# Transposing x by crossbar DMA instead of on TensorE, in a two-stage attention and MoE kernel

## Chip, cores and metric

The kernel runs on one core of one Trainium2 chip. The metric is the device time of one execution in microseconds (us), given as the median of a few runs. A profile is one further execution, recorded by the hardware profiler.

## The reference

Attention against 32 inducing points in two steps, then a dense expert layer with a hard swish. The four batches have 12480 rows of 128 channels each; the hidden width of the expert layer is 2048.

```python
B, N, m, C = (4, 12480, 32, 128)
scale = 1.0 / np.sqrt(C)
I = np.broadcast_to(inducing[None], (B, m, C))

def mab(q, kv):
    s = scale * (q @ kv.transpose(0, 2, 1))
    s = s - s.max(-1, keepdims=True)
    a = np.exp(s)
    a /= a.sum(-1, keepdims=True) + 1e-09
    return a @ kv
h = mab(I, x)               # 32 rows per batch, gathered from all of x
y = mab(x, h)               # every row of x looks at the 32 rows
# expert layer on the B*N rows of y: d_model 128, d_ff 2048
hid = y @ w_in
g = hid * np.clip(hid + 3.0, 0.0, 6.0) / 6.0
out = (g @ w_out).astype(np.float32)
```

## The kernel before

**The work.** Each batch of x is cut into seven groups: six of 128 x 16 rows (512 KB once they are bf16, 1 MB as fp32) and a last one of 48 x 4 rows. A group holds four chunks of 512 rows (the last group one), so a batch has 25 chunks. For each batch there are three parts:

- *a*, over groups: read x, cast it to bf16 (`a_cast`, L251, ScalarE, two halves per group), transpose it on TensorE in two halves into PSUM (`a_T`, L260) and copy that to the long bf16 tile `xT` on VectorE (L261), compute the scores against the inducing points and their exponentials (`a_s1`, L268 and L274), and add the weighted rows into `hnd` (`a_agg`, L282).
- *c*, once per batch: turn the 32 gathered rows into coefficients of the output stage (`c_units`: L470, L481, L490 and others).
- *b*, over chunks: for every row exponentials against coefficients (`b_base`, L652 and L659), a product with the tile `d` (`b_prod`, L668), 16 matmuls per chunk (`b_quad`, L692), one more (`b_lin`, L676), a row factor (`b_r`, L612 and L613), and the scaled result (`b_evac`, L708), which is stored once per group (L715). The tile `d` of a chunk comes from a packed tile `dk` of its group by a small DMA that copies 32 partitions to 128 (`b_spread`, L639).

**The order.** It is written by hand (`manual_schedule`), so each engine runs its instructions in the order in which the program emits them. Batch 0's parts *a* and *c* run first (`a_first`, `c_first`). Then a loop runs over all 100 chunks; while it does part *b* of batch b it takes small pieces of parts *a* and *c* of batch b+1 from a list. The list is filled at the first chunk of a batch, by `a_units(b + 1)` followed by `c_units(b + 1)`, and emptied evenly over 25 chunks: three times per chunk `bg(part)` takes as many units as the share of the chunks done asks for. For batch 1 four empty units stand ahead. So parts *a* of batches 1, 2 and 3 fall into the first third or so of the loop over batches 0, 1 and 2. A full group has five units: first half of the transposes with half of the next group's cast, half of the aggregation of the group before, second half of the transposes with the other half of the cast, the rest of the aggregation, and the scores. The casts of a batch's group 0 are emitted near the end of the batch before.

**Queues.** Loads of x and of the weights are issued by GpSimd (L118, L149 to L152). The spreads of `d` (L639, emitted four chunks ahead of their output and used by `b_prod` three loop turns later) and the outputs (L715) are issued by SyncE (SP). A load of x waits until its fp32 buffer (five of them) is free.

**Buffers.** `xT` has two tiles (one per batch in turn), the bf16 copy `xb` two (one per group in turn), `d` four. The PSUM tile of the transposes comes from `psF`, five banks that most of the work shares (for batch 0 it alternates with `psO`).

**The end.** Counts taken on the way say whether the fast form of the computation was valid. If not, a slow direct path runs under `tc.If` (L818 to L822). With the inputs given it doesn't run: every engine loads the flag, branches at L821 and goes past its instructions.

Of the kernel before, what the change touches and what calls it, by code (L numbers as in the profile page):

```python
# [9 lines left out]
FP32 = mybir.dt.float32  # L10
# [30 lines left out]
def kernel(  # L41
# [8 lines left out]
    nc = tc.nc  # L50
    P = nc.NUM_PARTITIONS
    B, N, C = x.shape
# [4 lines left out]
    scale = 1.0 / math.sqrt(C)  # L57


    groups = []  # L60
    t0 = 0
# [14 lines left out]

    keep = ctx.enter_context(tc.tile_pool(name="keep", bufs=1))
    bad_i = keep.tile([1, 1], I32, name="bad_i")

    with ExitStack() as es:  # L80
        es.enter_context(tc.manual_schedule())
# [70 lines left out]
            nc.gpsimd.dma_start(w_out_r[:, :, :], w_out)  # L152


        ident = const.tile([P, P], FP32, name="ident")
        make_identity(nc, ident[:, :])
        for g in range(1, XBUF):
            load_x(0, g)
# [94 lines left out]
        def a_T(b, g, h):  # L253
# [6 lines left out]
                nc.tensor.transpose(pt[:, (i - lo) * p : (i - lo + 1) * p], xb[:p, i, :], ident_b[:p, :p])  # L260
            nc.vector.tensor_copy(st["xT"][:, t0 + lo * p : t0 + hi * p], pt[:, : (hi - lo) * p])  # L261

        def a_s1(b, g):
            t0, p, n = groups[g]
            st = S[b]
            s1 = side_bank(b, [P, 512], FP32, "s1")
            for i in range(n):
                nc.tensor.matmul(  # L268
                    s1[:p, i * M : (i + 1) * M],
                    lhsT=st["xT"][:, t0 + i * p : t0 + (i + 1) * p],  # L270
                    rhs=I_T[:, :],
                )
# [29 lines left out]

        def a_units(b):

            us = []
            late = []
            for g in range(NGR):
                box = {}

                def s1_unit(g=g, box=box):  # L310
                    a_s1(b, g)
                    box["a1"] = S[b]["a1"]

                def first(g=g):
                    a_T(b, g, 0)
                    if g + 1 < NGR:
                        a_cast(b, g + 1, ((nc.scalar.copy, 0, 2),))

                def second(g=g):
                    a_T(b, g, 1)  # L320
                    if g + 1 < NGR:
                        a_cast(b, g + 1, ((nc.scalar.copy, 2, 4),))

                us.append(first)
                if late:
                    us.append(late.pop(0))
                us.append(second)
                us += late
                us.append(s1_unit)
                late = [  # L330
                    lambda g=g, box=box: a_agg(b, g, 0, box["a1"]),
                    lambda g=g, box=box: a_agg(b, g, 1, box["a1"]),
                ]
            return us + late
# [484 lines left out]
        bad_i[0:1, 0:1], min_val=0, max_val=1, skip_runtime_bounds_check_because="a comparison gives 0 or 1"  # L819
    )  # L820
    with tc.If(bad > 0, preferred_fallthrough_block=False):  # L821
        direct_path(tc, x, inducing, moe_w_in, moe_w_out, out, scale)  # L822


def direct_path(tc, x, inducing, moe_w_in, moe_w_out, out, scale):
    nc = tc.nc
    P = nc.NUM_PARTITIONS
    B, N, C = x.shape
# [7 lines left out]
    with ExitStack() as es:  # L836
        kp = es.enter_context(tc.tile_pool(name="d_keep", bufs=1))
        wk = es.enter_context(tc.tile_pool(name="d_work", bufs=1))
        ps = es.enter_context(tc.tile_pool(name="d_ps", bufs=1, space=PSUM))
        ident = kp.tile([P, P], FP32, name="d_ident")  # L840
        make_identity(nc, ident[:, :])
        w_in = kp.tile([P, F], FP32, name="d_w_in")
        nc.sync.dma_start(w_in[:, :], moe_w_in[:, :])
        w_out = kp.tile([P, FB, C], FP32, name="d_w_out")
# [19 lines left out]
            nc.tensor.matmul(s[:M, :TN], lhsT=I_T[:, :], rhs=xT[:, :])  # L864
            return s

        for b in range(B):
            mx = kp.tile([M, 1], FP32, name="d_mx")
            nm = kp.tile([M, 1], FP32, name="d_nm")
            D = kp.tile([M, 1], FP32, name="d_D")  # L870
            Ha = kp.tile([M, C], FP32, name="d_Ha")
            HT = kp.tile([P, M], FP32, name="d_HT")
            nc.vector.memset(mx[:, :], -3.0e38)
            nc.vector.memset(D[:, :], 0.0)
            nc.vector.memset(Ha[:, :], 0.0)
            with tc.For_i(b * N, (b + 1) * N, TN) as row:
                xt, xT = load(row)
                s = weights_of(xT)
                m1 = wk.tile([M, 1], FP32, name="d_m1")
                nc.vector.tensor_reduce(m1[:, :], s[:M, :TN], axis=AX.X, op=ALU.max)  # L880
                nc.vector.tensor_max(mx[:, :], mx[:, :], m1[:, :])
            nc.vector.tensor_scalar_mul(nm[:, :], mx[:, :], -scale)
            with tc.For_i(b * N, (b + 1) * N, TN) as row:
                xt, xT = load(row)
                s = weights_of(xT)
                a = wk.tile([M, TN], FP32, name="d_a")
                nc.scalar.activation(a[:, :], s[:M, :TN], ACT.Exp, scale=scale, bias=nm[:, 0:1])
                d1 = wk.tile([M, 1], FP32, name="d_d1")
                nc.vector.tensor_reduce(d1[:, :], a[:, :], axis=AX.X, op=ALU.add)
                nc.vector.tensor_add(D[:, :], D[:, :], d1[:, :])  # L890
                tr = ps.tile([P, 512], FP32, name="d_tr")
                nc.tensor.transpose(tr[:TN, :M], a[:, :], ident[:M, :M])
                aT = wk.tile([TN, M], FP32, name="d_aT")
                nc.vector.tensor_copy(aT[:, :], tr[:TN, :M])
                hp = ps.tile([P, 512], FP32, name="d_h")
                nc.tensor.matmul(hp[:M, :C], lhsT=aT[:, :], rhs=xt[:, :])
                nc.vector.tensor_add(Ha[:, :], Ha[:, :], hp[:M, :C])
            nc.vector.tensor_scalar_add(D[:, :], D[:, :], 1.0e-9)
            nc.vector.reciprocal(D[:, :], D[:, :])
            nc.vector.tensor_scalar_mul(Ha[:, :], Ha[:, :], D[:, 0:1])  # L900
            tr = ps.tile([P, 512], FP32, name="d_tr")
            nc.tensor.transpose(tr[:, :M], Ha[:, :], ident[:M, :M])
            nc.vector.tensor_copy(HT[:, :], tr[:, :M])
            with tc.For_i(b * N, (b + 1) * N, TN) as row:
                xt, xT = load(row)
                s = ps.tile([P, 512], FP32, name="d_s")
                nc.tensor.matmul(s[:TN, :M], lhsT=xT[:, :], rhs=HT[:, :])
                m2 = wk.tile([TN, 1], FP32, name="d_m2")
                nc.vector.tensor_reduce(m2[:, :], s[:TN, :M], axis=AX.X, op=ALU.max)
                nc.vector.tensor_scalar_mul(m2[:, :], m2[:, :], -scale)  # L910
                a = wk.tile([TN, M], FP32, name="d_a2")
                nc.scalar.activation(a[:, :], s[:TN, :M], ACT.Exp, scale=scale, bias=m2[:, 0:1])
                d2 = wk.tile([TN, 1], FP32, name="d_d2")
                nc.vector.tensor_reduce(d2[:, :], a[:, :], axis=AX.X, op=ALU.add)
                nc.vector.tensor_scalar_add(d2[:, :], d2[:, :], 1.0e-9)
                nc.vector.reciprocal(d2[:, :], d2[:, :])
                nc.vector.tensor_scalar_mul(a[:, :], a[:, :], d2[:, 0:1])
# [22 lines left out]
                nc.sync.dma_start(out[bass.ds(row, TN), :], ot[:, :])  # L940


# [28 lines left out]
```

## Time and profile before

| | us |
|---|---|
| runs: median (lowest to highest) of 3 | 327.13 (325.17 to 327.18) |
| profiled execution | 323.27 |
| its span, first to last instruction | 321.5 |
| TensorE busy | 299.8 |
| VectorE busy | 237.5 |
| ScalarE busy | 229.4 |
| ScalarE casts of full groups (L251), 42 | 43.4 |
| VectorE copies of transposes (L261), 48 full ones | 32.2 |
| TensorE transposes (L260), 384 full ones, by record | 29.4 |

The busy time of an engine is the time in which at least one of its instructions is on record as running; matmuls overlap in the records, so the sum of their single times is more than the time that they hold TensorE. PE stands for TensorE, PEld for its weight loads, DVE for VectorE, ACT for ScalarE, POOL for GpSimd and SP for SyncE; a q behind the name means its instruction queue (waits, branches, DMA issues). A row of a group reads "line engine operation out<-in count | busy us, mean ns". The loop over chunks starts at about 46 us; batches 0, 1 and 2 take 74, 74 and 73 us of it, and batch 3, beside which nothing is prepared, 46 us. The last output is issued at 313.77 us.

### The profile page before, as it was taken

The page shows a single profiled execution, that of the slowest core. Times are in us where ns is not written, and L with a number is a line of the kernel's source. Part 1 is how long each engine was busy: PE and PEld are TensorE (multiplying, and loading weights), DVE is VectorE, ACT ScalarE, POOL GpSimd, SP SyncE. Part 2 cuts the span into 40 slices and gives each one's busy share as a digit, 9 for nine tenths or more (in the row PEclk, how much of TensorE's full clock was granted, in tenths as well). Part 3 has the DMA queues.
Part 4 walks back from the last instruction along what each step waited for, and adds up shares of the span by engine and source line. Part 5 has one row for each costly group of instructions (what it writes and reads, how often), then busy time and mean ns, then how long its engine had stood idle before and what let it go on. Part 6 is the DMA issues. An engine that isn't in the chain of part 4 may idle for free.

```text
span 321.5 us, 9629 instructions
## 1 busy us (share of the span) xinstructions
PE 299.8 (93%) x3934; PEld 234.7 (73%) x3934; DVE 237.5 (74%) x542; ACT 229.4 (71%) x416; POOL 23.3 (7%) x59
## 2 busy tenths in 40 slices
PE   7798998999999998999899998999999999999980
PEld 2695756888677877888678777898777777777760
DVE  2688677788876768788786767797895777878780
ACT  2481789986689669986589759887589757777630
POOL 8150110201000000110000000100000000000000
PEclk9599999999999999999999999999999999999996
DMA  7999399898946444799965345652455246666652
GB/s 222 420 276 272 76 386 329 281 307 285 406 115 197 149 151 98 196 357 332 322 203 181 117 106 178 177 181 77 137 187 191 68 139 210 204 207 197 199 218 75
DMA packets 26487, 67.78 MB, mean 211 GB/s; under 512 B 5153, under 2 KB 19521, under 8 KB 20289
## 3 DMA queue, kind: packets, MB, share of 16 engines
q1 hardware_dynamic: 18160, 38.36, 37.1%
q0 software_dynamic: 8272, 28.71, 29.1%
q8 instruction: 33, 0.54, 0.7%
q14 instruction: 22, 0.17, 0.2%
HBM read 29.77 MB, written 25.56 MB: 172 GB/s over the span
## 4 chain that ended last, share of the span: by engine, by line
PE 75%; DMA 11%; DVE 6%; ACT 3%; issue 2%; POOL 0%; DVEq 0%; POOLq 0%
PE op L692 26%; PE bp L652 12%; DMA d<-dk 8%; PE op L676 6%; PE hnd L282 6%; PE pt L260 5%; PE cp L490 4%; PE dpm L470 4%; DMA xr<-in_x_dram 4%; PE s L268 3%; PE pp L623 2%; DVE xT L261 2%; PE sp L593 2%; PE ep L579 2%; DVE TD L668 1%
## 5 line engine op out<-in xcount | busy, mean ns | idle before, releaser
L659 ACT ACTIVATE TF<-bp 128x512 bf16<-128x512 f32 (+1 forms) x200 | 117.9, 600 | 34.8 <-PE rp L612 21.2
L692 PE MATMUL op<-Cq,TF 128*128 128x128 bf16 (+1 forms) x800 | 109.2, 223 | 0.0
L692 PE MATMUL op<-Cq,TD 128*128 128x128 bf16 (+1 forms) x800 | 106.3, 219 | 0.7 <-DVE TD L668 0.5
L708 DVE TENSOR_TENSOR os<-op,r_all 128x512 f32<-128x512 f32 (+1 forms) x100 | 68.2, 682 | 20.1 <-PE op L692 19.2
L692 PEld LDWEIGHTS <-TF 128*128 128x128 bf16 (+1 forms) x800 | 50.7, 98 | 33.5 <-issue 25.4
L652 PE MATMUL bp<-xT,W 128*128 128x512 bf16 (+1 forms) x200 | 75.1, 376 | 0.0
L668 DVE TENSOR_TENSOR TD<-TF,d 128x1024 bf16<-128x1024 bf16 (+1 forms) x100 | 66.8, 668 | 5.2 <-DMA d<-dk 2.5
L692 PEld LDWEIGHTS <-TD 128*128 128x128 bf16 (+1 forms) x800 | 61.4, 98 | 1.2 <-DVE TD L668 1.0
L676 PE MATMUL op<-BD,nf 128*128 128x512 f32 (+1 forms) x100 | 53.1, 531 | 0.0
L251 ACT CAST xb<-xr 128x1024 bf16<-128x1024 f32 (+1 forms) x47 | 46.0, 1002 | 7.1 <-DMA xr<-in_x_dram 7.1
L481 ACT ACTIVATE sq<-dpm 128x512 bf16<-128x512 f32 x60 | 36.5, 645 | 5.6 <-PE dpm L470 3.7
L261 DVE COPY xT<-pt 128x1024 bf16<-128x1024 bf16 (+1 forms) x56 | 33.8, 616 | 7.6 <-PE pt L260 7.5
L613 DVE RECIPROCAL r_all<-rp 128x4 f32<-128x4 f32 (+1 forms) x100 | 17.7, 177 | 23.9 <-PE rp L612 23.5
L612 PE MATMUL rp<-one,nf 128*128 128x4 f32 (+1 forms) x100 | 34.3, 343 | 0.1
L260 PE MATMUL pt<-ident_b,xb 128*128 128x128 bf16 (+1 forms) x400 | 31.0, 223 | 2.0 <-DVE xb L251 1.5
L282 PE MATMUL hnd<-xr,a 128*32 128x128 f32 x384 | 31.8, 229 | 0.5 <-ACT a L274 0.5
L282 PEld LDWEIGHTS hnd<-xr,a 128*32 128x32 f32 x384 | 25.6, 111 | 2.7 <-issue 2.1
L260 PEld LDWEIGHTS <-xb 128*128 128x128 bf16 (+1 forms) x400 | 24.6, 100 | 3.9 <-DVE xb L251 1.6
L118 POOL DMA_DIRECT2D xr<-in_x_dram x25 | 13.5, 543 | 161.8 <-ACT TF L659 94.4
L490 PE MATMUL cp<-w_out_b,sq 128*128 128x128 bf16 x256 | 24.3, 220 | 0.4 <-ACT sq L481 0.4
L470 PE MATMUL dpm<-dH,w_in_b 128*128 128x512 bf16 x64 | 23.7, 381 | 0.9 <-DVE dH L400 0.5
L630 ACT ACTIVATE dk<-pp 128x512 bf16<-128x512 f32 (+1 forms) x28 | 15.8, 564 | 11.5 <-PE pp L623 10.5
(106 smaller groups left out, 343.7 us busy)
## 6 DMA issues: line engine op xcount, KB each, us to landing
out_dram<-os SPq DMA_DIRECT2D x24, 1024.0 KB, 4.2
xr<-in_x_dram POOLq DMA_DIRECT2D x23, 1024.0 KB, 7.8
d<-dk SPq DMA_DIRECT2D x96, 128.0 KB, 4.1
xr<-in_x_dram POOLq DMA_DIRECT2D x2, 512.0 KB, 4.7
w_in_r<-in_moe_w_in_dram POOLq DMA_DIRECT2D x1, 1024.0 KB, 10.1
w_out_r<-in_moe_w_out_dram POOLq DMA_DIRECT2D x1, 1024.0 KB, 14.4
w_in_b<-in_moe_w_in_dram POOLq DMA_DIRECT2D x1, 512.0 KB, 6.8
w_out_b<-in_moe_w_out_dram POOLq DMA_DIRECT2D x1, 512.0 KB, 12.3
```

Source lines behind the costliest of these rows:

```text
L251: eng(xb[:p, lo:hi, :], xs[(b, g)][:p, lo:hi, :].bitcast(FP32))
L260: nc.tensor.transpose(pt[:, (i - lo) * p : (i - lo + 1) * p], xb[:p, i, :], ident_b[:p, :p])
L261: nc.vector.tensor_copy(st["xT"][:, t0 + lo * p : t0 + hi * p], pt[:, : (hi - lo) * p])
L282: nc.tensor.matmul(st["hnd"][:M, :C], lhsT=a1[:p, i * M : (i + 1) * M], rhs=xs[(b, g)][:p, i, :], start=(g == 0 and i == 0), stop=(g == NG ...
L470: nc.tensor.matmul(dpm[:, :], lhsT=w_in_b[:, jb * P : (jb + 1) * P], rhs=st["dH"][:, :, :, :, :].rearrange("p q k m i -> p (q k m i)"),)
L490: nc.tensor.matmul(st["cp"][:, k * C : (k + 1) * C], lhsT=sq[:, k * P : (k + 1) * P], rhs=w_out_b[:, jc, :], start=(jc == 0 and k == 0), s ...
L652: nc.tensor.matmul(bp[:, :w], lhsT=st["W"][:, k].rearrange("p m i -> p (m i)"), rhs=st["xT"][:, c0 : c0 + w],)
L659: nc.scalar.activation(st[("x", c)][:, k, :w], bp[:, :w], ACT.Exp, scale=scale)
L668: nc.vector.tensor_mul(u[:, :, :w], t[:, :, :w], d[:, :w].unsqueeze(1).to_broadcast([P, 2, w]))
L676: nc.tensor.matmul(op[:p, :], lhsT=st[("nf", g)][:, j * p : (j + 1) * p], rhs=st["BD"][:, :], start=True, stop=False, skip_group_check=True,)
L692: nc.tensor.matmul(op[:p, s * C : (s + 1) * C], lhsT=T[k][:, s * p : (s + 1) * p], rhs=st["Cq"][:, k, :], start=False, stop=(s == SL - 1 a ...
L708: nc.vector.tensor_mul(ot[:p, j * SL : (j + 1) * SL, :], op[:p, :].rearrange("p (s c) -> p s c", c=C), r_all[:p, b, c, :].unsqueeze(2).to_ ...
```

## The change

For batches 1 to 3, `a_T` and its copies are no longer called. A new function `a_X` issues one DMA per group on SP that reads the bf16 copy, transposes it in the DMA crossbar and writes `xT` directly. The transfer of group g+1 is issued in the unit that computes the scores of group g; that of group 0 is the batch's first unit, with two empty units behind it. The halves of the casts become units of their own. A batch has 83 units instead of 80. Batch 0 keeps its transposes on TensorE.

The direct path at the end is written with a loop over batches instead of four copies of its body, and it uses the identity matrix of the main path, which moves to the pool that outlives it, instead of making its own.

```diff
     keep = ctx.enter_context(tc.tile_pool(name="keep", bufs=1))
     bad_i = keep.tile([1, 1], I32, name="bad_i")
+    ident = keep.tile([P, P], FP32, name="ident")
...
-        ident = const.tile([P, P], FP32, name="ident")
         make_identity(nc, ident[:, :])
...
+        def a_X(b, g):
+
+            t0, p, n = groups[g]
+            nc.sync.dma_start(
+                S[b]["xT"][:, t0 : t0 + n * p].rearrange("c (i p) -> c i p", p=p),
+                xbs[(b, g)][:p, :n, :].rearrange("p i c -> p (i c)"),
+                transpose=True,
+            )
+
...
-            us = []
+            us = [lambda: a_X(b, 0), lambda: None, lambda: None]
             late = []
             for g in range(NGR):
                 box = {}
...
                 def s1_unit(g=g, box=box):
                     a_s1(b, g)
                     box["a1"] = S[b]["a1"]
-
-                def first(g=g):
-                    a_T(b, g, 0)
                     if g + 1 < NGR:
-                        a_cast(b, g + 1, ((nc.scalar.copy, 0, 2),))
-
-                def second(g=g):
-                    a_T(b, g, 1)
+                        a_X(b, g + 1)
+
+                for h in (0, 2):
                     if g + 1 < NGR:
-                        a_cast(b, g + 1, ((nc.scalar.copy, 2, 4),))
-
-                us.append(first)
-                if late:
-                    us.append(late.pop(0))
-                us.append(second)
-                us += late
+                        us.append(lambda g=g, h=h: a_cast(b, g + 1, ((nc.scalar.copy, h, h + 2),)))
+                    if late:
+                        us.append(late.pop(0))
                 us.append(s1_unit)
...
-        direct_path(tc, x, inducing, moe_w_in, moe_w_out, out, scale)
+        direct_path(tc, x, inducing, moe_w_in, moe_w_out, out, ident, scale)
...
-        ident = kp.tile([P, P], FP32, name="d_ident")
-        make_identity(nc, ident[:, :])
...
-        for b in range(B):
+        with tc.For_i(0, B * N, N) as r0:
...
-            with tc.For_i(b * N, (b + 1) * N, TN) as row:
-                xt, xT = load(row)
+            with tc.For_i(0, N, TN) as row:
+                xt, xT = load(r0 + row)
```

(The last four lines stand for the three loops of the direct path, which change alike.)

More of the change, by code (lines that the diff above doesn't have):

```diff
@@ L821, with direct_path @@
     with tc.If(bad > 0, preferred_fallthrough_block=False):
-        direct_path(tc, x, inducing, moe_w_in, moe_w_out, out, scale)
-def direct_path(tc, x, inducing, moe_w_in, moe_w_out, out, scale):
+        direct_path(tc, x, inducing, moe_w_in, moe_w_out, out, ident, scale)
+def direct_path(tc, x, inducing, moe_w_in, moe_w_out, out, ident, scale):
     nc = tc.nc
@@ L882, in direct_path @@
             nc.vector.tensor_scalar_mul(nm[:, :], mx[:, :], -scale)
-            with tc.For_i(b * N, (b + 1) * N, TN) as row:
-                xt, xT = load(row)
+            with tc.For_i(0, N, TN) as row:
+                xt, xT = load(r0 + row)
                 s = weights_of(xT)
@@ L903, in direct_path @@
             nc.vector.tensor_copy(HT[:, :], tr[:, :M])
-            with tc.For_i(b * N, (b + 1) * N, TN) as row:
-                xt, xT = load(row)
+            with tc.For_i(0, N, TN) as row:
+                xt, xT = load(r0 + row)
                 s = ps.tile([P, 512], FP32, name="d_s")
@@ L939, in direct_path @@
                 nc.vector.tensor_copy(ot[:, :], op[:TN, :C])
-                nc.sync.dma_start(out[bass.ds(row, TN), :], ot[:, :])
+                nc.sync.dma_start(out[bass.ds(r0 + row, TN), :], ot[:, :])
 _INS = ['x', 'inducing', 'moe_w_in', 'moe_w_out']
```

## The prediction, made before the changed kernel was run

> **What bounds the kernel now.** I read the page's busy rows first, then a table of stretches, then the chain of waits inside one stretch, then the queue that carries the new transfers.
>
> ```profile
> PE 299.8 (93%) x3934; PEld 234.7 (73%) x3934; DVE 237.5 (74%) x542; ACT 229.4 (71%) x416; POOL 23.3 (7%) x59
> ...
> DMA  7999399898946444799965345652455246666652
> ```
>
> TensorE leads, but these are averages. The loop works on batch b and prepares b+1 in its first third, so the second view is the stretches in which batches 1, 2 and 3 are prepared (columns: length, busy time and count of PE, PEld, DVE, ACT, POOL, granted clock, DMA share, GB/s).
>
> ```profile
> 52.00:76.00 24.00, 23.99 (x388) 20.67 (x389) 18.98 (x38) 20.97 (x34) 2.67 (x5) 1.00 0.87 273
> 127.00:150.00 23.00, 23.00 (x377) 19.64 (x376) 18.73 (x39) 18.74 (x32) 2.98 (x6) 1.00 0.83 272
> 201.00:230.00 29.00, 28.64 (x443) 23.86 (x442) 23.38 (x51) 21.76 (x37) 1.03 (x2) 1.00 0.50 154
> ```
>
> TensorE has no gap in any of them. ScalarE is next: 20.97/24, 18.74/23 and 21.76/29, or 87, 81 and 75%. VectorE stands at 79 to 81%. The DMA engines are crowded in the first two (0.87, 0.83), where x is loaded, and half free in the third. The chain of waits shows what TensorE does there.
>
> ```profile
> 128.79 0.39 PE s L268 x16
> 129.18 0.23 PE op L692 x4
> 129.41 0.45 PE pt L260 x8
> 129.86 0.22 PE bp L652
> ...
> 131.75 0.45 PE pt L260 x8
> ```
>
> Every piece starts where the last ends: this is issue-bound TensorE, so an instruction taken out here is time. Eight transposes cost 0.45 us (56 ns each), not the 225 ns that a single record shows, since records overlap. From the timeline, the scores (L268) of five full groups of the third stretch start at 202.69, 207.96, 212.99, 217.60 and 223.29: 5.15 us per group. Last, the transfers.
>
> ```profile
> out_dram<-os SPq DMA_DIRECT2D x24, 1024.0 KB, 4.2
> xr<-in_x_dram POOLq DMA_DIRECT2D x23, 1024.0 KB, 7.8
> d<-dk SPq DMA_DIRECT2D x96, 128.0 KB, 4.1
> ```
>
> SP's queue carries the spread of d and the outputs; the transposes join both there.
>
> **What the Trainium skill says.** DMA: Bandwidth & Descriptors, section Latency and other measured facts, gives a DMA transpose 261 GB/s with a non-contiguous middle dimension and 350 to 400 GB/s contiguous. No transfer of this trace is a transpose, so it neither agrees nor differs. The same page, section Issuing engines are not separate DMA queues, says that transfers of all issuers run on the same 16 engines. The trace agrees: with loads from POOL and spreads from SP both open the DMA share is 0.87. Runtime: NRT & Kernel Launch, section Instruction fetch mechanics, says that a taken branch with its target outside the fetched window waits for a fetch. The trace agrees:
>
> ```profile
> L821 PEldq COMPARE_BRANCH  x2: 95/1948/3801, 314.5 to 314.8; - x2
> ...
> L966 POOLq DRAIN  x3: 50/107/2832, 317.8 to 321.2; - x3
> ```
>
> The jump over the unused direct path takes TensorE 3.8 us, and ten instruction packets are moved after 315 us. POOL takes its branch at 314.5 and starts its drain at 317.8.
>
> **The change, part by part.**
>
> *Transposes off TensorE.* Per batch six groups of 16 and one of four go, 100 in all: 100 x 56 ns = 5.6 us, 16.8 us for three batches. Their waits go too, and two psF banks per group stay free. What is late next is ScalarE. A stretch of about 30 us would shrink to 24.4, and ScalarE works about 0.81 x 30 = 24.3 us in it: the two meet. At the start of each stretch ScalarE already leads (4.48 of 4.50 us at 122 to 126.5, TensorE 3.58), so the gain isn't whole. I take 4.0 us per batch, 12 us in all; the ends are 2.5 and 5.6.
>
> *Copies off VectorE.* Twelve L261 copies at 685 ns and two at 202 ns go per batch, 8.6 us. VectorE isn't the bound, so this counts nothing by itself; it also removes the handover TensorE to VectorE to TensorE ahead of the scores.
>
> *Casts on ScalarE.* The same two per group, 1.04 us each, now in units of their own. No time. The bf16 slot (two of them) is freed when its transfer has landed instead of when TensorE has read it.
>
> *The transfers.* Seven per batch on SP: six of 512 KB, one of 48 KB. Each waits on SP for the two casts of its group; spreads and outputs queue behind it. The wait itself should be nothing: the cast of one group ended at 206.90, and its scores' place in TensorE's order is at 212.99, so a transfer has 5 to 6 us, or 4.5 to 5.5 when groups come faster. If TensorE stalls on one group, the casts of the next don't depend on that, so two can be in flight. The latency: a spread of 128 KB landed in 2.5 us at the least, and its 128 packets of 1 KB at 46 ns fill 16 engines for 0.37 us, so 2.1 us are fixed. The data of 512 KB: bounded below by the spread's rate, 4 x 0.37 = 1.5 us; bounded above by the slowest kind of packet of the same size as a source row of a 128 x 128 block, 256 B, where w_out_b's load shows 41 ns each: 2048 x 41 / 16 = 5.2 us. I take the skill's 261 GB/s, 2.0 us, because it is the one figure for the same operation. Quiet landing: 2.1 + 2.0 = 4.1 us, hidden. Beside a load, with half the engines' turns, 6.1 us; behind a 1 MB output (128 KB takes 0.37 us, the output 2.6 us) 8.7 us. Two outputs and six groups fall in each stretch. In the two crowded ones I count one group 3.5 us late and the others saved by what is ahead, less what the stall lets ScalarE catch up: 2.5 us lost per crowded batch, 5 us in all; the ends are 0 and 12. In the third nothing is late.
>
> *The spread of d behind the transfers.* It is issued three chunks before VectorE needs it, some 9 us. Median landing 4.1 us leaves 5 us of cover for a transfer ahead of it (2 to 4 us). The cover is thin in one place: a spread issued at 149.55 took 9.40 us and was waited for. I put that inside the 5 us above. How long SP itself is held by one transpose the trace doesn't show: at least the 0.54 us of a spread's issue, at most the whole data time; by the same cover either costs nothing until it passes 5 us.
>
> *First transfer of a batch.* It is issued in the first unit and used six units later (a unit is 73.5 us / 80 = 0.92 us): 5.5 us, hidden. Batch 1's has four empty units more, which it needs, since 46 to 54 us run at a DMA share above 1. The 83 units for 80 only pack the third two thirds of the loop denser.
>
> *The short direct path.* It isn't executed. One loop body stands for four, so the jump lands nearer. Without any fetch, POOL's drain would begin 3.2 us sooner; I take 2.0 us, ends 0 and 3.3. The identity made once in another pool is made at the same place: nothing.
>
> *Sum.* -12 + 5 - 2 = -9 us, against the profiled execution's 323.27: 314.3 us. The median of the runs, 327.13, stands 1.2% above that execution; the same step from it gives 327.13 x 314.3 / 323.27 = 318.0 us. Changes below 1% (3.3 us) can't be told from none here.
>
> **Rivals.**
>
> *A, the forecast:* transfers mostly hidden, ScalarE next: 318.0 us, its own range 312 to 322.
>
> *B, gain eaten by crowding:* the loads, spreads and transfers share engines that are 0.83 to 0.87 busy in two of three stretches. A load of 1 MB (128 packets of 8 KB at 376 ns on 16 engines: 3.0 us), 1.5 spreads (0.6), 0.4 of an output (1.0) and one transfer (2.0) make 6.6 us of DMA work in a group of 5.15. For it: the sum passes the interval. Against: loads of the next batch have the 44 us without transfers to catch up, and the queues take turns. If the crowded batches lose all of their 8 us and the third keeps its 4, with the jump's 2: -6 + 4 for late spreads = -2 us, 325 us.
>
> *C, slower: the transfer is expensive and SP's ring becomes the bound.* Place: the wait of L268 for xT, every group. Price: with 3.6 us of data per transfer instead of 2.0 and half of a load taking turns, 1.6 + 3.6 + 1.5 = 6.7 us per group against 5.15 in the crowded stretches: 1.55 x 6.25 x 2 = 19 us, nothing gained in the third, less 2 for the jump: +17, 344 us. At the upper bound of 5.2 us it is 8.3 us there and 6.8 in the third: 3.15 x 12.5 + 1.65 x 6.25 - 2 = 48 us, 375 us. It decides from about 2.7 us per transfer. For it: the 41 ns packets, and VectorE: DVE Perf Modes, section The three transpose paths, prices one 128 x 128 block at 1309 ns by DMA against 390 ns on TensorE (this trace: 56 ns in a row). Against: that single block is mostly fixed latency, by the 2.1 us above.
>
> *D, hardly any transpose is late and the jump is nearly free:* 16.8 - 1 + 3.3 = 19 at the very most; with ScalarE's limit -14, 313 us.
>
> **How the numbers follow.** A 0.45, D 0.14, B 0.13, C 0.28. A and D are faster by over 1%, save a tenth of A that ends above 324; B is the middle; C slower, save a little. Faster 0.57, same 0.14, slower 0.29. The range starts at 311, below D, and reaches to 346, which takes in C at its middle price and leaves out its upper part; the likeliest case's own range is above.
>
> **What would show it.** Right: no L260 or L261 for batches 1 to 3 and 300 fewer matmuls; transfers of xT landing in 4 to 6 us; the scores 4.3 to 4.7 us apart in the third stretch, ScalarE there above 85%; short waits of L268 for a DMA near an output in the first two. The jump at L821 under 1 us. Wrong: PE waiting at L268 for the DMA in every group, with landings of 7 us and more, or spreads of d waited for in most groups (C); intervals unchanged at 5.1 us (B); SP held for several microseconds by one transpose, so that the waits show on the spread and not on xT.

## The result, and the profile after

The changed kernel takes 419.05 us in the median of four runs (411.23 to 431.58), the kernel before 327.15 on the same chip. Runs fall into a faster and a slower state, and here and below medians take all runs and ratios the faster ones alone (411.23 and 414.60 us of the changed kernel), while the profiles of e_short_path, e_loads_later and e_batch3 show slower runs and may make their loops some us too long. By the ratio the changed kernel takes 1.2647 times as long (95% interval 1.2486 to 1.2809). The profiled execution's span grew from 321.5 to 412.8 us. These are the page's lines after the change.

```profile
PE 302.4 (73%) x3634; PEld 230.9 (56%) x3634; DVE 217.3 (53%) x500; ACT 227.8 (55%) x416; POOL 23.3 (6%) x59
...
PEclk9699968655965599998967869998788999999998
DMA  7896995998999664448997945449997353557563
...
q1 hardware_dynamic: 56272, 47.95, 53.0%
...
PE 55%; DMA 33%; DVE 5%; ACT 4%; issue 2%; POOL 0%; SPq 0%; DVEq 0%; ACTq 0%; POOLq 0%
...
L277 PE MATMUL s<-I_T,xT 128*128 128x32 bf16 (+1 forms) x400 | 15.4, 182 | 94.3 <-DMA xT<-xb 92.1
```

Three hundred matmuls are gone, and yet TensorE's busy time rose by 2.6 us while its share of the span fell to 73%: it stands idle, and it also ran at a lower granted clock (the PEclk row has many slices at 5 to 8 tenths; the mean is 0.859). The last line carries the loss: the scores (L277 here, L268 before) were waited for 94.3 us, 92.1 of them for the DMA from xb to xT, in ten waits. TensorE's idle time grew by 88.7 us; with the 2.6 us more of busy time that is the difference of 91.3 us in span.

The trace, asked for the tile xT, gives the spread of the new transfers (durations in ns, minimum, median, maximum; what a DMA_TRANSPOSE lasts on SPq is the time for which it holds SP's instruction queue; a transfer lands when its completion is signalled):

```profile
L266 SPq DMA_TRANSPOSE xT<-xb x21: 1758/3006/16782, 49.3 to 318.8; - x21
...
DMA to landing us min/median/max: 3.3/7.4/30.8
```

The 3.3 us belong to a last group of 48 KB; the quickest transfer of 512 KB landed after 4.3 us, close to the forecast of 4.1, and the slowest took 30.8 us. The chain of waits between 60 and 100 us shows one of these, from issue to landing, and the table of stretches what the core did meanwhile:

```profile
68.11 28.57 DMA xT<-xb
...
96.72 0.61 PE s L277 x16
```

```profile
66.00:99.00 33.00, 6.55 (x91) 5.25 (x89) 4.57 (x10) 6.32 (x11) 1.62 (x3) 0.63 1.13 142
```

In 33 us TensorE was busy for 6.55. The DMA engines count as fully busy (1.13) and move only 142 GB/s. In the stretch from 52 to 76 us of the kernel before they moved 273 GB/s at a share of 0.87.

The following table places the loss. A loop over a batch is measured from the batch's first row factor (DVE, `r_all`) to the next batch's; the last one to the last scaled result (`os`), and the end from there to the end of the span. All are taken from the traces of single profiled executions.

| kernel | loop 0 | loop 1 | loop 2 | loop 3 | end |
|---|---|---|---|---|---|
| before | 77.1 | 74.1 | 73.2 | 46.9 | 7.8 |
| after | 140.5 | 96.8 | 81.2 | 46.7 | 4.9 |
| difference | +63.4 | +22.7 | +8.0 | -0.2 | -2.9 |

With 0.3 us before loop 0 the sum is +91.3. Loop 0's figure is the loosest: in e_short_path, e_batch3 and e_batch23 below, which have TensorE's transposes in that loop as before, it took 82.4, 84.9 and 82.7 us.

Loop 2, beside which the least is loaded, shows the milder form of the loss. In the table of stretches:

```profile
285.00:290.00 5.00, 1.87 (x28) 1.72 (x28) 0.18 (x1) 1.38 (x4) 0.00 (x0) 0.63 0.88 176
286.50:293.00 6.50, 4.87 (x47) 4.00 (x48) 1.81 (x4) 3.45 (x5) 0.00 (x0) 0.50 0.91 174
290.00:295.00 5.00, 5.00 (x57) 4.02 (x56) 2.63 (x6) 3.42 (x5) 0.56 (x2) 0.69 0.80 150
295.00:300.00 5.00, 5.00 (x85) 4.07 (x82) 2.95 (x7) 4.74 (x8) 0.47 (x1) 1.00 0.97 285
```

The scores wait 4.70 us for batch 3's first transfer, from 283.4 to 288.1 us. From 286.5 to 293 us the granted clock is 0.50; by 295 us it is 1.00 again. The same matmul of 128x512 (`bp`) takes 618 ns on average from 288.2 to 293 us and 381 ns from 295 to 300. A wait of 4.7 us thus costs more than itself. The same happens from 303 us, behind an output.

The end of the program, by contrast, went as the shorter code lets expect. These are the instructions of L822, the branch, and of the launch's last line:

```profile
L822 PEldq COMPARE_BRANCH  x2: 95/200/304, 408.6 to 408.9; - x2
```

```profile
L965 POOLq DRAIN  x3: 51/107/2813, 409.2 to 412.5; - x3
```

TensorE's branch takes 0.3 us instead of 3.8, and POOL's drain starts 0.5 us after its branch instead of 3.3.

### The profile page after: what moved, and what is told of

The parts are those of the page before. It is cut to its first block, busy times and chain, and to the rows that moved or that the text cites. A ratio compares the mean times of both kernels' runs of the same rounds, so it can differ in the third digit from the quotient of the medians.

```text
span 412.8 us, 9036 instructions
## 1 busy us (share of the span) xinstructions
PE 302.4 (73%) x3634; PEld 230.9 (56%) x3634; DVE 217.3 (53%) x500; ACT 227.8 (55%) x416; POOL 23.3 (6%) x59
## 4 chain that ended last, share of the span: by engine, by line
PE 55%; DMA 33%; DVE 5%; ACT 4%; issue 2%; POOL 0%; SPq 0%; DVEq 0%; ACTq 0%; POOLq 0%
DMA xT<-xb 29%; PE op L693 19%; PE bp L653 9%; PE hnd L291 5%; PE op L677 5%; PE cp L491 3%; PE dpm L471 3%; PE s L277 2%; PE pp L624 2%; DMA xr<-in_x_dram 2%; DMA d<-dk 1%; ACT TF L660 1%; ACT xb L251 1%; PE ep L580 1%; PE pt L260 1%
## 5 line engine op out<-in xcount | busy, mean ns | idle before, releaser
L693 PE MATMUL op<-Cq,TF 128*128 128x128 bf16 (+1 forms) x800 | 113.3, 231 | 0.0
L693 PE MATMUL op<-Cq,TD 128*128 128x128 bf16 (+1 forms) x800 | 110.6, 227 | 0.3 <-DVE TD L669 0.3
L277 PE MATMUL s<-I_T,xT 128*128 128x32 bf16 (+1 forms) x400 | 15.4, 182 | 94.3 <-DMA xT<-xb 92.1
L653 PE MATMUL bp<-xT,W 128*128 128x512 bf16 (+1 forms) x200 | 79.5, 398 | 0.3 <-ACT TF L660 0.3
L283 ACT ACTIVATE a<-s 128x512 fp32r<-128x512 f32 (+1 forms) x28 | 15.5, 554 | 98.0 <-PE s L277 97.9
L277 PEld LDWEIGHTS <-xT 128*128 128x128 bf16 (+1 forms) x400 | 12.8, 100 | 96.7 <-DMA xT<-xb 93.8
L693 PEld LDWEIGHTS <-TD 128*128 128x128 bf16 (+1 forms) x800 | 65.0, 103 | 0.7 <-DVE TD L669 0.6
L251 ACT CAST xb<-xr 128x1024 bf16<-128x1024 f32 (+1 forms) x47 | 46.7, 1010 | 7.0 <-DMA xr<-in_x_dram 7.0
L291 PE MATMUL hnd<-xr,a 128*32 128x128 f32 x384 | 36.2, 248 | 2.2 <-ACT a L283 2.2
L304 DVE TENSOR_TENSOR dacc<-dacc,a 128x512 f32<-128x512 f32 (+1 forms) x23 | 14.5, 631 | 34.5 <-ACT a L283 34.3
L291 PEld LDWEIGHTS hnd<-xr,a 128*32 128x32 f32 x384 | 29.7, 125 | 4.6 <-ACT a L283 3.4
## 6 DMA issues: line engine op xcount, KB each, us to landing
w_in_r<-in_moe_w_in_dram POOLq DMA_DIRECT2D x1, 1024.0 KB, 10.1
```

Source lines behind the costliest of these rows:

```text
L251: eng(xb[:p, lo:hi, :], xs[(b, g)][:p, lo:hi, :].bitcast(FP32))
L277: nc.tensor.matmul(s1[:p, i * M : (i + 1) * M], lhsT=st["xT"][:, t0 + i * p : t0 + (i + 1) * p], rhs=I_T[:, :],)
L291: nc.tensor.matmul(st["hnd"][:M, :C], lhsT=a1[:p, i * M : (i + 1) * M], rhs=xs[(b, g)][:p, i, :], start=(g == 0 and i == 0), stop=(g == NG ...
L653: nc.tensor.matmul(bp[:, :w], lhsT=st["W"][:, k].rearrange("p m i -> p (m i)"), rhs=st["xT"][:, c0 : c0 + w],)
L693: nc.tensor.matmul(op[:p, s * C : (s + 1) * C], lhsT=T[k][:, s * p : (s + 1) * p], rhs=st["Cq"][:, k, :], start=False, stop=(s == SL - 1 a ...
```

## Experiments

**Transfers alone, first try.** A kernel with DMAs only, three of each kind per stretch (arguments shortened at the dots):

```diff
+            nc.sync.dma_start(dst..., src..., transpose=True)          # turn, 512 KB
+            nc.gpsimd.dma_start(ld..., x[0, ...])                      # load, 1 MB, 8 KB packets
+            nc.sync.dma_start(pad[i][:, :, :128], src[:, :, :])        # copy, 512 KB, 256 B packets
+        for steps in ((turn,), (load,), (turn, load), (copy,), (copy, load), (store, turn), ...):
```

> A kernel of transfers alone, in nine stretches one after the other, three transfers of each kind in each: 512 KB transposes on SP; 1 MB loads of x on GpSimd in 8 KB packets; both together; plain copies of 512 KB in 256-byte packets on SP; these beside the loads; 1 MB stores and transposes in turn on SP's queue; transposes beside loads in 512-byte packets; transposes beside 1 MB stores issued by ScalarE; the loads in 512-byte packets alone. It computes nothing of the reference. Theory 1 (transposes and a transfer of another ring hold each other up): alone three transposes land within 9 to 10 us and three loads within 9 to 12; together 30 us or more, far above the sum of about 19; the plain copies beside the loads take about the sum, since only the crossbar ties the engines together; stores and transposes of one queue take about the sum, 17. Theory 2 (many small packets lose their turns to 8 KB packets): the plain copies beside loads are slowed as the transposes are, and loads in 512-byte packets slow nothing. Theory 3 (an output ahead in SP's own ring is what delays): the stretch of stores and transposes is the slow one, and transposes beside loads take about the sum.

Most stretches weren't apart: the loads of the second began at 5.79 us, beside the transposes of the first (5.43). Two of them did run by themselves and are taken up under m_apart, the same kernel with full barriers.

**The short direct path alone.** The kernel before, with only the direct path's part of the change.

```diff
-        for b in range(B):
+        with tc.For_i(0, B * N, N) as r0:
...
-            with tc.For_i(b * N, (b + 1) * N, TN) as row:
+            with tc.For_i(0, N, TN) as row:
```

> The kernel before with the short direct path alone; transposes stay on TensorE. From the two traces the stretch after the last scaled result is 7.8 us before and 4.9 after, so every theory expects 2.9 us less than before: 324.2 us for a median of 327.1. If the shorter end belonged to something else in the change, 327.

Measured: 325.13 us in the median of 20 runs against 328.17, ratio 0.9882 (0.984 to 0.9924). The end is 4.8 us, as in the changed kernel. So this half of the change gains some 1.2%, and the whole loss belongs to the other half, the transposes.

**No loads after batch 0.**

```diff
         def load_x(b, g, parts=1):
             t0, p, n = groups[g]
+            if b:
+                xs[(b, g)] = xs[(0, g or 5)]
+                return
```

> The changed kernel without the loads of x for batches 1 to 3 (they use rows of batch 0 that are still in the buffers, so the output isn't the reference's); transposes, spreads and outputs stay. Theory 1 (transposes beside loads): the loops over batches 0 and 1, 140.5 and 96.8 us in the changed kernel, shrink to about the 81.2 of batch 2, beside which there are few loads: 412.8 - 59 - 16 = 338 us in the profile, 340 to 345 median. Theory 2 (each transpose costs 4 us or more of its ring in any case) and theory 3 (outputs ahead in the ring): 400 us or more.

Measured: 338.75 us (336.85 to 340.55), ratio 1.0328. Loops 87.9, 79.7 and 78.6. All 21 transfers land after 3.4 to 6.5 us:

```profile
DMA to landing us min/median/max: 3.4/4.6/6.5
```

In the spans of the profiles (338.8 us here) 74 of the 91.3 us are gone, about as theory 1 expected. What makes the transfers slow in this kernel is loads beside them, not their own price and not the outputs ahead of them, which are all still there.

**Loads held back.**

```diff
+        def load_late(b):
+            seen = cst.tile([P, 1], BF16, name="seen")
+            nc.gpsimd.tensor_copy(seen[:, :], S[b]["xT"][:, N - 1 : N])
+            while held:
+                load_x(b + 1, held.pop(0))
...
             elif b + 1 < B:
-                load_x(b + 1, g - (NGR - XBUF))
+                held.append(g - (NGR - XBUF))
...
-            return us + late
+            return us + late + [lambda: load_late(b)]
```

> The changed kernel with the loads for the next batch but one held back until the last transpose of a batch has landed; the one 1 MB load that the batch itself still needs stays where it is. Nothing is left out. Theory 1: the loop over batch 1 falls from 97 to about 88 us, that over batch 0, beside whose start five loads of batch 1 are still open, from 140 to about 110: 370 to 380 us. Theory 3: no change, 413 us and more.

Measured: 367.65 us (365.3 to 374.79), ratio 1.1202; loops 104.1, 89.8 and 82.8. The longest landing fell from 30.8 to 10.1 us, where theory 3 expected no change. With one load of 1 MB per stretch left, the long transfers are gone, and the loss that one load leaves (9 to 10 us of landing beside it) is still there.

**Transfers alone, with barriers.** The kernel above with two sweeps of VectorE over all tiles between the stretches.

> Transfers alone again, now with a full barrier between the stretches (in m_transfers the loads of one stretch began beside the transposes of the one before), three of each kind per stretch: transposes; loads; transposes and loads; 256-byte copies; copies and loads; stores; stores and transposes; loads in 512-byte packets; transposes and these; transposes and stores issued by ScalarE; stores, transposes and loads; spreads and transposes; spreads, transposes and loads; all four. Sums from the quiet prices: a transpose 2.4 us, a load 3.0, a store 2.6, a spread 0.4, each stretch with some 2 us of fixed latency. Theory 1 (the crossbar ties the 16 engines together, so that a transpose beside another ring's packets goes at the pace of whichever engine is busy with them): transposes and loads 25 us or more against a sum of 18; copies and loads about 18. Theory 2 (small packets lose turns): copies and loads as slow as transposes and loads. Theory 3 (only a mixture with stores in the same ring crawls): transposes and loads about 18, stores, transposes and loads 40 or more against a sum of 26.

Times from the table of stretches (length, busy DVE and POOL, clock, DMA share, GB/s), here transposes, loads, both; then copies, and copies with loads:

```profile
5.50:14.00 8.50, 0.26 (x12) 0.00 (x0) 1.00 0.92 171
15.60:25.50 9.90, 0.14 (x6) 1.73 (x3) 1.00 0.84 318
27.20:44.70 17.50, 0.43 (x12) 1.60 (x3) 1.00 1.02 270
45.70:54.50 8.80, 0.18 (x7) 0.00 (x0) 1.00 0.80 179
55.60:72.50 16.90, 0.28 (x7) 1.60 (x3) 1.00 1.04 279
```

Transposes and loads together take 17.5 us, the sum of 8.5 and 9.9 less some latency, and copies with loads 16.9. All four kinds of transfer together took 28.8 us. Theories 1 and 3 as they stood were contradicted, and theory 2's loss isn't seen either. Here, though, all loads were issued at once, before a transpose had moved. And the two stretches of m_transfers that ran by themselves took longer with the same transfers: from the first issue to the last landing, transposes and loads 20.8 us against 17.8 here, transposes beside stores issued by ScalarE 24.1 against 17.7. The times of such mixtures aren't fixed, and what decides them wasn't found.

**Plain copies in place of the transposes, in the kernel.**

```diff
+            if n == TG:
+                for k in range(2):
+                    nc.sync.dma_start(
+                        S[b]["xT"][:, t0 + k * 1024 : t0 + k * 1024 + 1024].rearrange("c (i p) -> c i p", p=p),
+                        xbs[(b, g)][:, k::2, :],
+                    )
+                return
```

> The changed kernel in which each transpose of a full group is a plain copy of the same bytes from the bf16 copy to xT on the same queue, in two halves with 256-byte pieces on the reading side (the values are therefore not transposed, and the output isn't the reference's). Loads, spreads and outputs as in the changed kernel. Theory 1 (crossbar): the loops over batches 0 and 1 fall to 85 to 90 us and 80, as without loads, and the whole to 345 us. Theory 2 (small packets beside 8 KB packets, whatever they do): 400 us or more, with landings over 15 us where loads run.

Measured: 374.58 us (one run), loops 105.8, 90.3 and 81.3, longest landing 12.7 us. Neither theory holds as put. Set against e_no_loads and the changed kernel, the profile of each giving one figure, loop 0's +63.4 splits into 10.8 without any load, 17.9 that plain copies of the same packets lose to loads, and 34.7 that only transposes lose. In loop 1 it is 5.6, 10.6 and 6.5; in loop 2, 5.4, 2.7 and nothing. The first share of loop 0 is the least certain, for the reason given under the table of loops: against 82 to 85 us it would be 3 to 6. Against e_tensor_no_loads below, TensorE's transposes without loads, it is 9.3, 6.5 and 5.5 in the three loops. Plain copies without loads were not run: the other two shares suppose that these cost what transposes cost without loads.

**A load that begins while transposes move.** Transfers alone, the loads issued one by one behind memsets on POOL.

```diff
+        stretch(sp=[turn] * 6)
+        stretch(sp=[turn] * 6, pool=[2, load])
+        stretch(sp=[turn] * 6, pool=[2, load, 1, load, 1, load])
+        stretch(sp=[copy] * 6, pool=[2, load, 1, load, 1, load])
...
+        stretch(sp=[store, spread, turn, spread, turn, spread, turn], pool=[load, 1, load, 1, load])
+        stretch(sp=[store, spread, copy, spread, copy, spread, copy], pool=[load, 1, load, 1, load])
```

> Transfers alone, eight stretches with full barriers. In m_apart all loads were issued together at the start, so that they had passed before a transpose moved; here a load is issued about 4 us after six transposes have begun, as in the loop over batch 0. Stretches: six transposes; the same with one load begun later; with three loads 2 us apart; six 256-byte copies with three such loads; six transposes with a load in 512-byte packets; with a store issued by ScalarE; a store, then three spreads and transposes in turn, with three loads 2 us apart; the same with copies. Sums: six transposes 16 us, three loads 9. Theory 1 (a load that begins while a transpose moves makes both crawl, the crossbar tying the engines together): six transposes with three later loads 45 us or more, with one load 25 or more, and six copies with three loads 25. Theory 2 (turns by packet, nothing else): all of them near their sums, 19 to 27 us. If only the stretch with a store and spreads crawls, the mixture in SP's ring is needed.

The stretches in this order (length, busy DVE, ACT, POOL, clock, DMA share, GB/s); the loads came 4 us apart, not 2:

```profile
7.80:23.30 15.50, 0.14 (x7) 0.00 (x0) 0.00 (x0) 1.00 1.03 192
25.30:45.10 19.80, 0.36 (x11) 0.00 (x0) 7.63 (x3) 1.00 1.05 206
47.10:83.30 36.20, 0.69 (x22) 0.00 (x0) 15.46 (x7) 1.00 1.12 174
83.30:109.30 26.00, 0.94 (x27) 0.00 (x0) 15.46 (x7) 1.00 0.92 242
...
153.00:188.90 35.90, 0.89 (x25) 0.00 (x0) 8.50 (x5) 1.00 1.09 172
188.90:210.00 21.10, 0.54 (x14) 0.00 (x0) 8.50 (x5) 1.00 1.02 292
```

Some of these stretches end up to 1.4 us before the last landing, others after it. From the first issue to the last landing six transposes take 16.9 us alone, 20.9 with one load and 35.6 with three; six copies with three loads take 25.0. At 3.0 us for a load the sums are 19.9 and 25.9: with one load the sum holds within 1.0 us, with three the copies keep to it and the transposes need 10 us more. In the mixture of the kernel it is 35.3 us with transposes against 21.0 with copies, and one of those transposes held SP's queue for 18.3 us. The two stretches left out of the table, transposes beside a load in 512-byte packets and beside a store issued by ScalarE, took 22.0 and 19.9 us. Each stretch ran once.

So the crawl is shown with transfers alone: same size of packets, same loads, 10 to 14 us more, with the transposing as the difference that was made. Theory 1's direction holds, its sizes (45 us with three loads, 25 with one) don't. The packets tell how the two cases differ. In the copies' stretch between 104 and 105 us the 16 engines moved 48 packets of 8 KB and 48 of 256 B, a small one in 0.03 us on average: the two queues take turns one for one, the load loses little, and a copy waits until the load is through. In the transposes' stretch between 63 and 64 us they moved 9 packets of 8 KB and 40 of 256 B, and a small packet took 0.36 us on average instead of the 0.022 of the transposes alone. But transposes don't always crawl beside a load: in m_apart, between 30 and 31 us, the engines moved 48 and 48 packets there too. Why they do in one case and not in the other, and whether the crossbar ties the engines to one another's pace, wasn't shown.

**No loads, and transfers two groups ahead.**

```diff
-        xbin = es.enter_context(tc.tile_pool(name="xbin", bufs=2))
+        xbin = es.enter_context(tc.tile_pool(name="xbin", bufs=3))
...
+            us = [lambda: a_X(b, 0), cast(1, 0), cast(1, 2), none, lambda: a_X(b, 1), none]
...
-                    if g + 1 < NGR:
-                        a_X(b, g + 1)
+                    if g + 2 < NGR:
+                        a_X(b, g + 2)
```

> As e_no_loads (no loads for batches 1 to 3), and casts and transposes run two groups ahead of the scores instead of one, with a third bf16 buffer. Without the lead the loops over batches 0 to 2 took 87.9, 79.7 and 78.6 us, 4.5 to 7 us more than on TensorE's transposes, in a profile of 338.8. Theory: what is left there is lateness alone (issue behind outputs and spreads on SP, landing after 4.2 to 6.5 us, and the clock lost after each wait), so a lead of two groups brings the loops to 69 to 71 us and the whole to 305 to 312. Rival: ScalarE, which does the casts in the same stretch, is the next bound, and the loops stay at 73 to 75: 318 to 325.

Measured: 320.4 us (317.28 to 322.25), ratio 0.9846 (0.9724 to 0.9967); 18 us less than e_no_loads, so lateness was most of what was left there. But the loops are 76.2, 74.0 and 72.5, not 69 to 71. The scores of loop 1 stand at 126.6, 132.2, 137.1, 141.5, 146.1 and 149.8 us: 4.64 us apart, against 5.3 before (122.7 to 149.2), so a group does get cheaper by some 0.7 us. The first of them comes 7.6 us into the loop, where the kernel before had it after 3.1, and that eats the five intervals' gain of 3.3.

**The control: TensorE's transposes, no loads.** e_short_path with the three lines of e_no_loads.

> The control for the two runs without loads: the kernel before with the short direct path and TensorE's transposes, and also without the loads of x for batches 1 to 3 (so the output isn't the reference's). e_no_loads_lead, with DMA transposes, no loads and a lead of two groups, took 320.4 us, loops 76.2, 74.0 and 72.5. Theory A (the removed transposes are worth next to nothing even where the DMA hides them, because ScalarE and the start of each stretch take the place): 319 to 324 us here, loops 76, 73.5 and 73. Theory B (they are worth some 3 to 5 us per batch, and loads cost the kernel before nothing): 325 us as e_short_path, and more than e_no_loads_lead by at least 4.

Measured: 320.25 us (318.33 to 322.13), ratio 0.9687 (0.9599 to 0.9775); loops 78.6, 73.2 and 73.1. In time that is e_no_loads_lead (320.4); in ratio to the kernel before on each one's own chip the control is 1.6% ahead, with intervals that just overlap. Either way, even with no load beside them and a lead of two groups, DMA transposes gained nothing over TensorE's. What the control gains over e_short_path, from which it differs in the loads alone, comes from leaving these out; the gain of e_no_loads_lead over the kernel before is no larger than the control's.

**Early start as well.** Batches 2 and 3 by DMA, no loads; the first two transfers are issued in the last chunk of the batch before.

```diff
+            casts = [(0, 0, -2), (0, 2, -1)] if b < XFROM else [(0, 0, -6), (0, 2, -5), (1, 0, -4), (1, 2, -3)]
...
+            if b >= XFROM:
+                ahead.setdefault((b - 1) * NCK - 1, []).append(
+                    lambda b=b: (a_begin(b), a_X(b, 0), a_X(b, 1))
+                )
```

> The upper bound of the idea for two batches: as e_batch3's early start and lead of two groups, transposes by DMA for batches 2 and 3, batch 1 on TensorE, no loads of x for batches 1 to 3 (so the output isn't the reference's). With one load in the stretch e_batch3's loop over batch 2 took 79.5 us, landings 13.1 and 10.6 us. Theory (that load is the whole loss): loops over batches 1 and 2 of 69 to 71 us, total 313 to 317. Rival (ScalarE bounds): 73 to 74, total 321 to 325.

Measured: 321.53 us (321.0 to 327.63), ratio 0.9738 (0.9634 to 0.9842); loops 1 and 2 of 73.3 and 75.8. The total is the rival's, loop 2 is longer than either expected, and the rival's reason isn't shown. For 12 us of loop 2 ScalarE is indeed busy all the time:

```profile
200.00:204.00 4.00, 4.00 (x65) 3.33 (x63) 2.42 (x6) 4.00 (x8) 0.00 (x0) 1.00 1.03 172
204.00:208.00 4.00, 4.00 (x70) 3.14 (x67) 3.01 (x6) 4.00 (x7) 0.00 (x0) 1.00 0.85 169
208.00:212.00 4.00, 4.00 (x55) 3.32 (x52) 3.11 (x8) 4.00 (x8) 0.00 (x0) 1.00 1.16 239
```

But TensorE is busy all the time there too. Where it does wait in the stretches that prepare batches 2 and 3 (119.5 to 152.9 and 192.8 to 228.5 us), it waits for transfers, with landings up to 7.4 us (us in total, times, longest):

```profile
PE s L281 <- DMA xT<-xb: 4.6, 2, 3.0
PE s L281 <- DMA xT<-xb: 6.4, 3, 2.9
```

For ScalarE itself it waits 0.2 us in each; how far ScalarE's casts, for which a transfer waits on SP, delay the transfers wasn't separated. The transposes that are gone were worth some 5.6 us per batch by the prediction's count, and these waits alone are of that size.

**Two versions meant to gain,** with all loads. Batch 3 alone by DMA with lead and early start (`XFROM = 3`); and batches 2 and 3, with batch 3's loads held back as in e_loads_later (`XFROM = 2`).

> A version for gain: short direct path, transposes by DMA for batch 3 alone, beside whose preparation one load of 1 MB and a small one run, issued two groups ahead of their scores, and those of its first two groups in the last chunk of the batch before. In e_no_loads_lead the groups came 4.64 us apart instead of 5.2, but its start was 4 us late, which ate the gain. Theory (lateness and loads are the whole loss, and 0.5 us per group is gained once both are gone): the loop over batch 2 takes 69 to 71 us instead of 73.2, so 0.979 to 0.985 of before. Rival: ScalarE bounds the stretch, loop at 73, 0.988 as e_short_path.

Measured: 329.52 us (324.99 to 333.42), ratio 1.0121 (0.9983 to 1.026). Loop 2 took 79.5 us. Neither expectation came true. Beside the one load of 1 MB in the stretch landings took 13.1 and 10.6 us, and a lead of two groups doesn't cover these.

> As e_batch3, but for batches 2 and 3, with the loads of batch 3 held back until the last transpose of batch 2 has landed; batch 1 stays on TensorE. Theory: a gain of 2 to 4 us in each of two loops and 2.9 at the end: 0.970 to 0.978 of before. Rival: the 1 MB load that falls into each of the two stretches costs as in e_loads_later (a landing of 9 us), and the loops are 74 and more: 0.99 or above.

Measured: 338.72 us (337.95 to 340.72), ratio 1.0458 (1.0367 to 1.055); loops 1 and 2 of 84.2 and 76.7, landings of 9.9 and 10.6 us beside the load, as the rival expected. Of the kernels that leave nothing out e_short_path remains the fastest.

## Why the prediction was wrong

*The removal of the transposes: -12 us forecast, about nothing measured.* TensorE's gap-free order was read rightly, and a group does come sooner when its transfer is mostly hidden (4.64 us in loop 1 without loads, inside the 4.3 to 4.7 that the prediction gave as the mark of success for the third stretch). The step that failed is taking 4.0 us per batch as free of new costs. The comparison of e_no_loads_lead with its control gives 320.4 against 320.25. What took the gain back, even without loads, are waits for transfers: 3.5 us in the first half of loop 1 of e_no_loads_lead, 4.6 and 6.4 in e_early_no_loads. For ScalarE itself, forecast as next, TensorE waited 1.3 and twice 0.2 us in the same stretches; what its casts do to the start of the transfers stays open. What the removal is worth with no wait at all wasn't measured.

*Quiet price of a transfer: nearly right.* 2.0 us of data and 4.1 us to landing were forecast; six transposes alone landed 2.5 us apart (512 KB in 2.5 us are 210 GB/s, not the 261 that the prediction took), and quiet landings in the kernel were 4.3 to 5 us. Behind an output 8.7 us was forecast, and the one issued at 299.80 landed after 8.11. Rival C's price of 3.6 to 5.2 us is too high for a quiet transfer; its place, the wait of the scores for xT, was the right one.

*Beside a load: 6.1 us forecast, up to 30.8 measured. This is the term that failed most.* The prediction took "half the engines' turns" as half the bytes. Turns are by packet (48 against 48 in one us of m_begun): with 256 B against 8 KB a transfer hardly moves until the load is through (12.7 us at the longest with copies, behind an output and loads). And for transposes loads that come one by one into a running series slow both (m_begun: 35.6 us against 25.0 for copies). The two crowded stretches were to lose 5 us together; they lost 63.4 and 22.7 where a gain was set against it.

*Cover of 5 to 6 us: wrong.* It was reckoned from the cast's end, as if SP stood ready. On SP the first transfer of batch 3 comes behind an output and a spread that wait for VectorE: it was issued at 282.70, and TensorE wanted its result at 283.4, so it was late by 4.70 although it landed after 5.38. The one issued at 299.80 left SP as its second cast ended (298.70 plus 1.07 us), behind an output, and was late by 4.61. In the third stretch, where "nothing is late" was forecast, the loop became 8.0 us longer.

*The clock: left out.* Around a wait of 4.7 us the granted clock stood at 0.50 for at least 6.5 us. Its mean was 0.981 before and 0.859 after. No term of the sum had this.

*The spread of d: inside the cover.* It was a small item; `d` is 1% of the chain after, against 8% before.

*The short direct path: right, and larger than forecast.* -2.0 was taken, ends 0 and 3.3; the end shrank by 2.9 us in the trace.

*The sum.* -12 + 5 - 2 = -9 against +63.4 + 22.7 + 8.0 - 2.9 and 0.1 of the rest, +91.3. Rival C's upper bound, 375 us, also fell short, because it priced the transfer and not what it and a load do to each other.

What stays open: by what mechanism transposes and loads slow each other, why one load alone and loads issued at once didn't show it (m_begun, m_apart), and how the loss in loop 0 divides exactly, since each share rests on single profiles.

## What to carry to other kernels

Before work is moved from an engine to the DMA queues, ask what else is open on those queues in that stretch and in which packet sizes: a transfer of small packets can wait for the whole of a load of large ones (copies landed after 4.3 us alone and up to 15.6 beside three loads in m_begun), and a transpose can slow the load too (16 to 18 us to landing in m_begun against 8 beside copies). Count the cover of a transfer from where its issuing queue reaches it, past everything in front, and price a new wait with the clock that it costs TensorE afterwards. Compare with a control that leaves out the same loads; without it the 0.9846 of e_no_loads_lead would have looked like a gain of the transposes.

## What the runs showed of the hardware

- A DMA_TRANSPOSE of 512 KB held SP's instruction queue for 1.3 to 5.5 us in the kernels without loads and for up to 18.3 us beside loads (m_begun), against 0.54 us for most spreads. Copies in 256-byte packets held it too, up to 3.0 us alone and 9.4 beside loads (m_apart). What stands behind on SP waits as long.
- Transposes of 512 KB landed about 2.5 us apart in a row (210 GB/s), plain copies in 256-byte packets 2.3 to 2.5 us apart. Three transposes with three loads took about the sum when the loads were issued at once (17.8 us in m_apart, though 20.8 in m_transfers), and six transposes with three loads one by one took 35.6 us against a sum of 25.9.
- The granted clock fell to 0.50 within a wait of 4.7 us, stayed there from 286.5 to 293 us, 5 us past the wait's end, and stood at 1.00 by 295; a 128x512 matmul took 618 ns meanwhile and 381 afterwards.
- A program that jumps over less code ended sooner: by 2.9 us of 7.8 with one copy of a loop body instead of four.
